# Four layers forward and backward on one core: the derivative of the feature map is no longer stored, and the opening's loads and zeroing are planned elsewhere

## The chip, the core and the metric

The kernel runs on one core of a Trainium2 chip, in one launch. The metric is the device time of that launch in microseconds (us), lower is better. TensorE is called PE here, VectorE DVE, ScalarE ACT, GpSimd POOL and SyncE SP, as the profile does; PEld is the weight load of PE. SP and ACT also issue the DMAs: SPq and ACTq are their issue queues.

## The reference

A residual stream x of 2048 tokens by 640 features (bf16) goes through four layers, A, B, A, B, and the gradient of the result goes back through them. Layer A is linear attention with 32 heads of 20 features, layer B is attention over a window of 256 keys.

```python
def _A_ref(x, wqkv, wo):                      # x is the layer norm of the stream
    q, k, v = split_heads(x @ wqkv)           # 32 heads of 20
    phi = lambda t: jnp.where(t > 0, t + 1, jnp.exp(t)) + 1e-6
    pq, pk = phi(q), phi(k)
    kv = einsum("bhsd,bhse->bhde", pk, v);  z = sum over s of pk
    o = (pq @ kv) / (pq . z + 1e-6)
    return merge_heads(o) @ wo
x = x + A(layernorm(x)); x = x + B(layernorm(x)); x = x + A(layernorm(x)); x = x + B(layernorm(x))
```

The outputs are the last x, and the gradients with respect to the input x, both weights of A and both weights of B (each pair of weights is used in two layers, so their gradients are sums of two). In the backward pass of layer A the gradient at phi(q) is multiplied by the derivative of phi at q, which is 1 where q is above 0 and exp(q) elsewhere, that is min(exp(q), 1); the same for k. Since phi(q) = max(q, 0) + min(exp(q), 1) + 1e-6 up to rounding, min(phi(q) - 1e-6, 1) is that derivative too.

## The kernel before, in words

The stream is cut into 16 tiles of 128 tokens (`TT` = 16), and everything is written as operations of one engine each. Each stage collects its operations in a list planner (`Sched`, lines 87 to 200): every operation names its engine, a cost in ns, what it reads and writes and, for a DMA, its kind and size. `order` (126) then plays the stage through with these costs. In each step it takes the operation that can start earliest, of equals the one that was created first, and that fixes the order of the instructions in every engine's queue. It fixes the order alone: on the chip each queue runs in that order and waits for what the data really needs. The planner's DMA model is in lines 167 to 177: one shared channel of 300 bytes per ns, plus 2000 ns to landing.

The stages, with the stretch of the profiled span that each takes:

- **Opening, 0 to about 120 us** (`forward`, 1056 to 1069, `a_first` at 963). For each of the 16 tiles: layer norm (`ln`, 471: two `bn_stats`, `bn_aggr` and the scaled write of tile `hn` on DVE, two small activations on ACT), transposition of hn on PE with a copy by ACT, and a store of hn to DRAM from SP (486). Then `a_qkv` (488) multiplies by the 1920 columns of `Wqkv_A` in six chunks of 320 (two for q, two for k, two for v; five matmuls each). For a q or k chunk ACT takes exp into tile `ee` (516), DVE takes the minimum with 1 in place (517) and adds max(q, 1e-6) to it (520); the sum is the feature `pp` or, for k, a slice of `gcar`. After that ee holds the derivative. ACT issues five stores of 160 KB per tile: pq (527), eq (529, the derivative of q), pk (533), ek (535, the derivative of k) and v (507). ee has four buffers, pp and hn's transpose two and three, and hn one.
- Before the first tile the queues hold the loads: on ACT Wqkv_A in two parts (chunks 0 and 1 first, 955 to 958), on SP the input x in three parts, tile 0, tiles 1 to 3, tiles 4 to 15 (959 to 961). In the same stage SP loads the other weights (`Wo_A`, `Wqkv_B`, `Wo_B`, five slices each, 1061 to 1064) and turns twenty weight blocks by DMA into DRAM copies for the backward pass (`flip_w`, 924 and 1065). Here the profile names `Wo_A` and `Wqkv_B` slabR, since they lie over that buffer, as hn and several later tiles do.
- DVE also zeroes fourteen tiles that later stages use (`zeros`, 407, written at 1059). In the planner nothing holds these back, so they can start at time 0.
- **First pass, about 120 to 400 us** (`ab_pass(0)`, 984): per tile the rest of layer A, layer B, and for the third layer hn, k and v (again with `a_qkv`, chunks 2 to 5, so with pk, ek and v stores). **Second pass, about 400 to 740 us** (`ab_pass(2)`): the same for the last two layers; q of the third layer comes late, in `late_q` (542), which stores pq (568) and eq (569).
- **Window attention backward**, about 740 to 1045 and 1470 to 1770 us (`B_attn_bwd`, 1613), in an order written out by hand; the change does not touch it.
- **Two backward phases**, `bwd_phase` (1091), about 1045 to 1470 and 1770 to the end. In the second half of each, `lin_grads` (1465) runs per tile, interleaved with `tail` (1276) of the same layer, and in the first phase with `local_dO` (1362) of the layer below. `lin_grads` loads eq and ek of its tile from DRAM (1476, SP queue, two buffers each; in the first phase ek's lie over slabR) and multiplies them with PE's result (1503). `tail` computes the layer norm's gradient: DVE 1317, ACT 1324 (w), POOL 1327 (gw = w + g), DVE 1329 (the new g). `local_dO` has a product on POOL too (1377), and DVE reduces it (1380).

The names that the prediction uses: the planner's dependency keys are tuples such as `("rs", 0, tt)` (the layer norm scale of tile tt is known) or `("vv", tt, 5)` (the last chunk of v is written). A key that nothing has written yet when the operation is created gives no dependency. That is the case for the weight loads of line 1064, which name `("vv", tt, 5)` before it exists; their only order is that of one slice behind the other of the same weight.

## Time and profile before

| what | value |
|---|---|
| three runs before | 2145.37, 2146.77, 2151.33 us, median 2146.77 |
| the profiled execution | 2145.22 us, its span 2143.5 us |
| mean granted PE clock | 0.975 |
| busy shares of the span | PE 94%, PEld 65%, DVE 67%, ACT 56%, POOL 41% |
| instructions | 68024 |
| moved by DMA | 376.43 MB |
| stores of eq and ek | 64, 160 KB each, all issued by ACT |
| loads of eq and ek | 64, 160 KB each, all issued by SP |

The profile is one execution, recorded by the hardware. A row of a timeline gives the start in us from the start of the span, the duration, engine, line, operation, output and input, and in brackets how long the engine had been idle and what ended that. A row of a group gives, after the bar, the busy time in us and the mean ns of one instruction, then the idle time just before them. A row of stretches gives start and end, then for each engine the busy us with the number of instructions, then the granted PE clock (1.00 is full), the share of the 16 DMA engines in use, and GB/s. The issue of a DMA is not counted as busy time of its engine.

### The profile page before, as it was taken

How to read it: one execution, taken by the hardware profiler on the slowest of the kernel's cores; microseconds unless marked ns; L12 is line 12 of the kernel's file. 1: busy time of each engine (PE TensorE's matmuls, PEld its weight loads, DVE VectorE, ACT ScalarE, POOL GpSimd, SP SyncE). 2: the span in 40 equal slices, each digit the busy share in tenths (PEclk: the TensorE clock that was granted, in tenths of full speed). 3: DMA queues.
4: the chain of work that ended last, by engine and by line, in shares of the span. 5: the costliest groups of instructions: out<-in, count | busy, mean ns of one | idle time of the engine just before them, and what ended most of it. 6: DMA issues, size and time to landing. Idle time of an engine off the chain costs nothing. (4 is left out here: it accounts for less than half of the span.)

```text
span 2143.5 us, 68024 instructions
## 1 busy us (share of the span) xinstructions
PE 2008.2 (94%) x27908; PEld 1389.2 (65%) x27908; DVE 1440.1 (67%) x2954; ACT 1203.3 (56%) x1995; POOL 879.4 (41%) x1850
## 2 busy tenths in 40 slices
PE   6879999889999899999899999999999999999999
PEld 4656666656666577777666667656777765666764
DVE  6757777567776599999634368606998984444651
ACT  3527878647888589899422233216988881221430
POOL 1015666316777456666223223204665652230210
PEclk9989999999999899999899999999999999999999
DMA  9928989469998788987987899847999998989943
GB/s 291 256 106 179 191 193 191 119 198 201 210 208 191 146 157 151 161 161 155 193 185 168 213 200 203 175 104 142 157 158 151 170 170 162 199 185 227 186 111 102
DMA packets 943687, 376.43 MB, mean 176 GB/s; under 512 B 821776, under 2 KB 923664, under 8 KB 943120
## 3 DMA queue, kind: packets, MB, share of 16 engines
q1 hardware_dynamic: 866176, 299.16, 71.9%
q10 hardware_dynamic: 77200, 72.94, 11.1%
q8 instruction: 218, 3.57, 0.7%
q14 instruction: 93, 0.76, 0.1%
HBM read 109.02 MB, written 112.07 MB: 103 GB/s over the span
## 5 line engine op out<-in xcount | busy, mean ns | idle before, releaser
L1693 DVE TENSOR_TENSOR ds_sb<-pair,e_sb 128x768 bf16<-128x768 f32 x480 | 437.6, 951 | 57.8 <-PE pair L1654 49.6
L1673 ACT ACTIVATE e_sb<-pair 128x768 bf16<-128x768 f32 x480 | 390.9, 815 | 95.6 <-PE pair L1654 67.4
L839 POOL TENSOR_SCALAR_AFFINE_SELECT e_sb<-e_sb 128x384 bf16<-128x384 bf16 (+1 forms) x512 | 198.3, 406 | 357.5 <-ACT e_sb L830 335.7
L830 ACT ACTIVATE e_sb<-s_ps 128x1152 bf16<-128x1152 f32 (+2 forms) x256 | 273.8, 1070 | 100.2 <-PE s_ps L826 78.4
L1685 POOL TENSOR_SCALAR_AFFINE_SELECT e_sb<-e_sb 128x256 bf16<-128x256 bf16 x448 | 182.0, 406 | 227.1 <-ACT e_sb L1673 226.9
L1327 POOL TENSOR_TENSOR gw<-w,gcar 128x640 f32<-128x640 f32 x64 | 89.4, 1397 | 423.4 <-ACT w L1324 406.8
L1138 PEld LDWEIGHTS <-slabR 128*128 128x128 bf16 x1920 | 185.6, 98 | 116.1 <-DMA slabR<-o 3.7
L1682 POOL TENSOR_SCALAR_AFFINE_SELECT e_sb<-e_sb 128x256 bf16<-128x256 bf16 x512 | 206.5, 406 | 89.3 <-ACT e_sb L1673 89.3
L1718 PEld LDWEIGHTS <-dsT 128*128 128x128 bf16 x2880 | 146.2, 97 | 97.7 <-issue 91.5
L1709 ACT COPY dsT<-dsT_ps 128x768 bf16<-128x768 bf16 x240 | 191.2, 796 | 9.4 <-PE dsT_ps L1706 6.6
L448 PE MATMUL mm_ps<-slabR,hnTB 128*128 128x320 bf16 x960 | 170.5, 308 | 10.5 <-DVE gcar L520 6.0
L1706 PE MATMUL dsT_ps<-ident,ds_sb 128*128 128x128 bf16 x1848 | 158.2, 223 | 1.3 <-ACT dsT L1709 1.1
L1722 PEld LDWEIGHTS <-ds_sb 128*128 128x128 bf16 x2880 | 145.1, 96 | 0.8 <-issue 0.8
L1722 PEld LDWEIGHTS <-e_sb 128*128 128x128 bf16 x2880 | 145.0, 96 | 0.0
L844 POOL TENSOR_SCALAR_AFFINE_SELECT e_sb<-e_sb 128x512 bf16<-128x512 bf16 x224 | 142.6, 636 | 0.0
L833 ACT ACTIVATE e_sb<-s_ps 128x384 bf16<-128x384 f32 (+2 forms) x256 | 119.9, 468 | 32.3 <-PE s_ps L826 15.1
L1138 PE MATMUL dw_ps<-dqkv,slabR 128*128 128x480 bf16 x640 | 134.7, 366 | 0.0
L1309 ACT ACTIVATE dh<-mm_ps 128x320 f32<-128x320 f32 x64 | 28.0, 437 | 189.8 <-PE mm_ps L1138 164.9
L1138 PE MATMUL dw_ps<-dqkv,om 128*128 128x480 bf16 x640 | 134.2, 366 | 0.0
L1654 PE MATMUL pair<-slabR 32*128 32x384 bf16 (+2 forms) x1024 | 120.5, 326 | 12.0 <-DVE ds_sb L1693 5.2
L1138 PEld LDWEIGHTS <-om 128*128 128x128 bf16 x800 | 77.5, 98 | 71.3 <-DMA om<-o 2.4
L864 PEld LDWEIGHTS <-e_sb 128*128 128x128 bf16 x2880 | 105.5, 96 | 26.6 <-POOL e_sb L844 7.5
(234 smaller groups left out, 4357.6 us busy)
## 6 DMA issues: line engine op xcount, KB each, us to landing
qkvp<-qk_slab SPq DMA_DIRECT2D x64, 256.0 KB, 3.7
hn<-slabR SPq DMA_DIRECT2D x64, 160.0 KB, 2.9
qkvp<-v_slab SPq DMA_DIRECT2D x32, 256.0 KB, 3.4
slabR<-qkvp SPq DMA_DIRECT2D x16, 512.0 KB, 4.8
o<-o SPq DMA_DIRECT2D x48, 160.0 KB, 2.9
eq<-ee ACTq DMA_DIRECT2D x32, 160.0 KB, 3.0
pq<-pp ACTq DMA_DIRECT2D x32, 160.0 KB, 2.4
ek<-ee ACTq DMA_DIRECT2D x32, 160.0 KB, 2.7
```

The costliest lines, as they stand in the source:

```text
L448: nc.tensor.matmul(ps.t[:, w0:w0 + width], lhsT=lhsT(), rhs=rhs(), start=start, stop=stop)
L830: op("ACT", av(3 * nkt * P), lambda: nc.scalar.activation(e.t[:, 0:3, 0:nkt, :], s3.t[:, :, 0:nkt * P].rearrange("p h (i q) -> p h i q", q=P),
L839: nc.gpsimd.affine_select(out=v, in_=v, compare_op=ALU.is_ge, fill=0.0, base=0, pattern=[[0, h1 - h0], [1, P]], channel_multiplier=-1)
L1138: nc.tensor.matmul(ps.t[:, w0:w0 + width], lhsT=lhsT(), rhs=rhs(), start=start, stop=stop)
L1673: nc.scalar.activation(E[n][:, 2 * p:2 * p + 2], PR[h][:, :, 0:3 * P].rearrange("p i (j q) -> p i j q", q=P), ACT.Exp, scale=self.c_att)
L1682: nc.gpsimd.affine_select(out=e[:, :, j, :], in_=e[:, :, j, :], compare_op=ALU.is_ge, fill=0.0, base=0, pattern=[[0, 2], [-1, P]], channel ...
L1685: nc.gpsimd.affine_select(out=e[:, :, j, :], in_=e[:, :, j, :], compare_op=ALU.is_ge, fill=0.0, base=-1, pattern=[[0, 2], [1, P]], channel ...
L1693: nc.vector.tensor_mul(DS[n][:, hs], PR.pop(h)[:, :, 0:3 * P].rearrange("p i (j q) -> p i j q", q=P), E[n][:, hs])
L1706: nc.tensor.transpose(ps[:, i, j, :], DS[n][:, 2 * p + i, j, :], self.ident)
L1709: (nc.scalar.copy if by == "A" else nc.vector.tensor_copy)(TSB[h], TPS.pop(h))
L1718: nc.tensor.matmul(a[:, 0, hh, :], lhsT=TSB[2 * n + hh // 2][:, hh % 2, j, :], rhs=ld[g]["K"][:, k, cs], start=(i == 0), stop=(i == len(dq ...
L1722: nc.tensor.matmul(a[:, 1 + x, hh, :], lhsT=src[n][:, hh, j, :], rhs=ld[g][rhs][:, q, cs], start=(i == 0), stop=(i == len(dkv) - 1))
```

## The change

Three edits, in the planner's input and in what is stored.

- **No eq and ek.** The two DRAM tensors per layer and their 64 stores (lines 529, 535, 569) are gone. In `lin_grads` the same two buffers are loaded from pq and pk, and POOL turns each in place into the derivative with one `tensor_scalar`: add -1e-6, then minimum with 1, over 128 x 640 bf16. The planner is told 1000 ns for it.
- **Opening's loads.** A third DMA kind "L" is told its landing time outright: x tile 0 at 2.8 us, Wqkv_A's parts at 5 and 9.5 us, x tiles 1 to 3 at 5.5 us, x tiles 4 to 15 at 14 us. The load of x tiles 4 to 15 moves behind the first LN store (hn of tile 0) in the plan, and the fifteen weight slices now name the LN store of tiles 1 to 11 (`("hnd", 0, tt)`), which is written by then.
- **Zeroing.** The fourteen memsets are created one after the other between tiles 3 and 13, and each names the layer norm scale of a tile from 3 to 12.

```diff
@@ line 166 @@
             ready[e].remove(o)
             if o.dma:
                 kind, size = o.dma
-                if kind == "B":
+                if kind == "L":
+                    free[e], chan_ = t + 500, size - 2000
+                elif kind == "B":
                     free[e], chan_ = t + 1300, t + 2500
                 elif kind == "T":
                     free[e] = t + 1100 + size / 1000
@@ line 174 @@
                 else:
                     free[e] = t + (330 if e == "SP" else 200)
                     chan = max(chan, t) + size / 300
-                o.end = (chan_ if kind == "B" else chan) + 2000
+                o.end = (chan_ if kind in "BL" else chan) + 2000
             else:
                 free[e] = t + o.dur
                 o.end = free[e] + (170 if e == "PE" else 0)
@@ line 273 @@
         for l in (0, 2):
             self.sv[l] = dict(
                 pq=d.tile([T, D], BF, name=f"pq{l}"), pk=d.tile([T, D], BF, name=f"pk{l}"),
-                eq=d.tile([T, D], BF, name=f"eq{l}"), ek=d.tile([T, D], BF, name=f"ek{l}"),
                 v=d.tile([T, D], BF, name=f"v{l}"), o=d.tile([T, D], BF, name=f"o{l}"),
                 r32=d.tile([T, self.H], F32, name=f"r32{l}"),
                 mbd=d.tile([D, D + P], BF, name=f"mbd{l}"),
@@ line 483 @@
                                                                  scalar2=rs, op0=ALU.subtract, op1=ALU.mult),
                    [("x", tt), m, ("rs", l, tt)], [hn])
                 turn(how, lambda: hnT.t, lambda: hn.t, DT, [hn], [key_of(hnT)])
-                dma("SP", lambda: self.tm_view(self.hn_d[l])[:, tt, :], lambda: hn.t, 160 * KB, [hn], [])
+                dma("SP", lambda: self.tm_view(self.hn_d[l])[:, tt, :], lambda: hn.t, 160 * KB, [hn], [("hnd", l, tt)])
 
             def a_qkv(l, tt, hnT):
                 sv = self.sv[l]
@@ line 521 @@
                             out=pd(), in0=ps.t[:, 0:CW], scalar=1e-6, in1=es(), op0=ALU.max,
                             op1=ALU.add), [ps, (e, ci)], [(c["p"], ci) if kind == "q" else ("pk", tt, ci)])
                         if ci == 3 and "q" in c:
-                            p_, e = c["p"], c["q"]
+                            p_ = c["p"]
                             turn("s", lambda: pqT[:, :, tt * P:(tt + 1) * P], lambda: p_.t, DT, [(p_, 0), (p_, 1)],
                                  [("pqT", tt)])
                             dma("ACT", lambda: self.tm_view(sv["pq"])[:, tt, :], lambda: p_.t, 160 * KB,
                                 [(p_, 0), (p_, 1)], [])
-                            dma("ACT", lambda e=e: self.tm_view(sv["eq"])[:, tt, :], lambda e=e: e.t, 160 * KB,
-                                [(e, 0), (e, 1)], [])
                         if ci == 3:
-                            e = c["k"]
                             dma("ACT", lambda: self.tm_view(sv["pk"])[:, tt, :], lambda: pk[:, tt, :], 160 * KB,
                                 [("pk", tt, 2), ("pk", tt, 3)], [])
-                            dma("ACT", lambda e=e: self.tm_view(sv["ek"])[:, tt, :], lambda e=e: e.t, 160 * KB,
-                                [(e, 2), (e, 3)], [])
                     return f
                 return [chunk(ci) for ci in range(6)]
 
@@ line 566 @@
                 else:
                     flip(own, lambda: p_.t, 160 * KB, [(p_, 0), (p_, 1)], [("pqT", tt)], **F)
                 dma("ACT", lambda: self.tm_view(sv["pq"])[:, tt, :], lambda: p_.t, 160 * KB, [(p_, 0), (p_, 1)], [], **F)
-                dma("ACT", lambda: self.tm_view(sv["eq"])[:, tt, :], lambda: e.t, 160 * KB, [(e, 0), (e, 1)], [], **F)
 
             def a_kv(l):
                 sv = self.sv[l]
@@ line 956 @@
                 dma("ACT", lambda c0=c0, c1=c1: wsb["Wqkv_A"][:, :, c0 * CW:c1 * CW],
                     lambda c0=c0, c1=c1: wA[:, :, c0 * CW:c1 * CW], 400 * (c1 - c0) * KB, [],
                     [("Wqkv_A", ci) for ci in range(c0, c1)])
-            for t0, t1 in ((0, 1), (1, 4), (4, TT)):
-                dma("SP", lambda t0=t0, t1=t1: x[:, t0:t1, :], lambda t0=t0, t1=t1: xin[:, t0:t1, :],
-                    160 * (t1 - t0) * KB, [("Wqkv_A", 0)] if t0 == 4 else [], [("x", i) for i in range(t0, t1)])
+                S.ops[-1].dma = ("L", 9500 if c0 else 5000)
+
+            def load_x(t0, t1, lands):
+                dma("SP", lambda: x[:, t0:t1, :], lambda: xin[:, t0:t1, :], 160 * (t1 - t0) * KB,
+                    [("hnd", 0, 0)] if t0 >= 4 else [], [("x", i) for i in range(t0, t1)])
+                S.ops[-1].dma = ("L", lands)
+            load_x(0, 1, 2800)
+            load_x(1, 4, 5500)
 
             def a_first(items, l, base, lag=0.0, late=()):
 
@@ line 1055 @@
 
             items = []
             a_first(items, 0, 0)
+            items.append((0.5, len(items), lambda: load_x(4, TT, 14000)))
             spread(items, 1.0, 9.0, [lambda f=f: op("POOL", 350, f, [], ["masks"]) for f in self.mask_steps])
-            spread(items, 2.0, 12.0, [lambda t=t, v=v, n=n: op("DVE", 100 + n * 0.45, lambda: nc.vector.memset(t, v), [],
-                                                               ["zeros"]) for t, v, n in zeros])
+            spread(items, 3.0, 13.0, [lambda t=t, v=v, n=n, i=i: op(
+                "DVE", 100 + n * 0.45, lambda: nc.vector.memset(t, v), [("rs", 0, 3 + i * 10 // len(zeros))], ["zeros"])
+                for i, (t, v, n) in enumerate(zeros)])
             for i, (k, src) in enumerate((("Wo_A", self.A_wo), ("Wqkv_B", self.B_wqkv), ("Wo_B", self.B_wo))):
                 for j in range(DT):
                     tt = 1 + 3 * i + j
-                    items.append((tt + 0.9, len(items), lambda k=k, src=src, j=j, tt=tt: load_w(k, src, "SP", j, [("vv", tt, 5)])))
+                    items.append((tt + 0.9, len(items), lambda k=k, src=src, j=j, tt=tt: load_w(k, src, "SP", j, [("hnd", 0, tt)])))
             for i in range(4 * DT):
                 at = 4.5 + 0.5 * i
                 items.append((at, len(items), flip_w(i, ("rs", 0, int(at) - 1))))
@@ line 1473 @@
                         c[nm] = b = R[nm].buf()
                         flip(lambda b=b: b.t, lambda src=src: src[row, :], size,
                              [("dNd", tt)] if nm == "dNT" else [], [b])
-                    c["eq"], c["ek"] = load("eq", sv["eq"], tt), load("ek", sv["ek"], tt)
+                    for nm, p_ in (("eq", "pq"), ("ek", "pk")):
+                        c[nm] = b = load(nm, sv[p_], tt)
+                        op("POOL", 1000, lambda b=b: nc.gpsimd.tensor_scalar(
+                            out=b.t, in0=b.t, scalar1=-1e-6, scalar2=1.0, op0=ALU.add, op1=ALU.min), [], [b])
 
                 def chunk(kind, ci):
                     def f():
```

## The prediction

> **What bounds the kernel now.** I read the page's busy shares first, then busy time by stretch, then the timelines of the two places that the change touches.
>
> ```profile
> PE 2008.2 (94%) x27908; PEld 1389.2 (65%) x27908; DVE 1440.1 (67%) x2954; ACT 1203.3 (56%) x1995; POOL 879.4 (41%) x1850
> ```
>
> ```profile
> 20.00:30.00 10.00, 9.37 (x58) 6.24 (x59) 6.15 (x19) 5.80 (x14) 0.00 (x0) 0.70 0.99 300
> 40.00:50.00 10.00, 7.27 (x58) 5.18 (x59) 6.20 (x18) 4.78 (x13) 0.00 (x0) 0.83 0.90 251
> 0.00:50.10 50.10, 30.82 (x215) 20.45 (x216) 31.98 (x89) 18.63 (x46) 5.89 (x26) 0.90 0.96 298
> 50.10:109.60 59.50, 50.99 (x467) 37.35 (x465) 43.03 (x123) 35.66 (x88) 0.00 (x0) 1.00 0.96 250
> 165.00:378.00 213.00, 201.31 (x3467) 140.93 (x3465) 160.82 (x405) 172.43 (x286) 139.00 (x306) 1.00 0.89 188
> 1245.00:1365.00 120.00, 113.62 (x1046) 86.18 (x1045) 101.25 (x218) 39.06 (x102) 36.48 (x27) 1.00 1.00 195
> 1950.00:2055.00 105.00, 102.37 (x1001) 79.63 (x1000) 66.32 (x174) 34.45 (x88) 16.09 (x12) 0.98 0.92 191
> ```
>
> The columns behind the length are PE, PEld, DVE, ACT, POOL, then granted clock, DMA share and GB/s. PE is the bound nearly everywhere: 94% of the span, 95% of the first pass (201.31 of 213), 95% and 97% of the two `lin_grads` halves (the last two rows). The opening is the exception. PE is busy 30.82 of the first 50.10 us and 50.99 of the next 59.50, with the DMA engines 96% in use. So the opening is where something can be won, and the backward halves, where POOL gets new work beside a busy DVE, are where something can be lost.
>
> ```profile
> 9.82 1.48 SPq L416 DMA_DIRECT2D hn<-slabR  x1
> ...
> 50.15 0.35 SPq L416 DMA_DIRECT2D hn<-slabR  x1
> ...
> 109.62 0.34 SPq L416 DMA_DIRECT2D hn<-slabR  x1
> ```
>
> These are the LN stores of tiles 0, 5 and 15, one per tile, so they give the pace: 40.3 us for the first five tiles (8.1 each), 59.5 us for the next ten (5.95 each).
>
> **The change, part by part.** *Opening, start.* DVE's first layer norm stands behind the zeroing:
>
> ```profile
> 2.33 1.66 DVE L1059 MEMSET mbd<- 128x1920 uint32 x1 [0.35 <-issue]
> 4.04 1.57 DVE L1059 MEMSET qk_slab<- 128x512 uint32 x3
> 5.66 2.11 DVE L1059 MEMSET v_slab<- 128x512 uint32 x4
> 7.68 0.43 DVE L476 BATCH_NORM_STATS2 st<-x 128x6 f32<-128x320 bf16 x1
> ```
>
> ```profile
> Wqkv_A<-in_A_wqkv_dram ACTq DMA_DIRECT2D x1, 1600.0 KB, 12.2
> ...
> x<-in_A_x_dram SPq DMA_DIRECT2D x1, 160.0 KB, 2.6
> ```
>
> Tile 0 of x is issued as the first DMA of SP at 0.8 and lands 2.6 later, at about 3.5 (estimate). From the first statistics (7.68) to the LN store (9.82) it takes 2.14 us, so with the zeroing gone from the front the store comes at about 5.6: **-4.2 us**. The weights must keep up. The second part of Wqkv_A took 12.2 us to land because the slices and all of x were issued around it. In the new order 3.1 MB (x tiles 0 to 3 and Wqkv_A) go first; at 298 GB/s that is 10.4 us, so k's columns are there at about 11, when the two q chunks (after 7) are just through. x tiles 4 to 15, moved behind the LN store, make it 5.1 MB, 17 us; tile 4 isn't due before 5.6 + 4 x 5.6 = 28. What hides the later load is thus ten us of earlier tiles; without that cover it would cost the difference.
>
> *Opening, tiles 0 to 5.* At the later pace these five take 29.7 us; they took 40.3, so 10.6 us are lost. Two idle gaps of PE and two stretches of low clock explain it:
>
> ```profile
> 20.11 0.71 PE L464 MATMUL s_ps<-ident,slabR 128*128 128x128 bf16 x5 [3.68 <-DVE slabR L482]
> ...
> 42.15 0.45 PE L464 MATMUL s_ps<-ident,slabR 128*128 128x128 bf16 x5 [2.85 <-DVE slabR L482]
> ```
>
> The gaps are 3.68 + 2.85, the clock cost 0.30 x 10 + 0.17 x 10 = 4.7 (rows 20 to 30 and 40 to 50), together 11.2. In both gaps PE waits for a layer norm (line 482) that DVE wrote late: its queue had statistics of later tiles in front, an order that the planner chose with wrong landing times. With landing times near the real ones and the weight slices spread over tiles 1 to 11 instead of the first third, I let three quarters go: **-8 us**. Bounds: 0 (the new order has gaps of its own) and -10.6.
>
> *Opening, tiles 5 to 15.* Per tile PE is busy 5.1 us of 5.95, DVE 4.3, ACT 3.6 plus five issues:
>
> ```profile
> L416 ACTq DMA_DIRECT2D eq<-ee x32: 326/422/1445, 15.0 to 654.7; - x32
> L416 ACTq DMA_DIRECT2D ek<-ee x32: 326/388/672, 23.6 to 422.8; - x32
> ```
>
> [...] Two of the five go, 0.8 us of a tile, part of which runs beside ACT's own work; and of the 14.9 MB that 250 GB/s moves in 59.5 us, twenty stores of 160 KB, 3.3 MB or 22%, go too. Against that stand the memsets, 1.66 + 1.57 + 2.11 and about 0.9 (estimate) for the fifth v_slab and five small ones, 6.2 us of DVE, eight tenths of them here: 0.5 per tile, DVE then 4.8. PE at 5.1 is the floor, so the bounds are -8.5 (all at the floor) and +5 (all memset time on the path, nothing won). I take a pace of 5.6, nearer the floor since three engines then stand at 5.1 or less: **-3.5 us**.
>
> *The two passes.* 32 further stores go, 16 of ek and 16 of eq, 12.8 us of ACT's queue at 0.4 each. PE leads here with 95%, so ACT's work hides it; the 11.7 us in which PE idles in the first pass bound the gain. But the planner replays the whole forward stage and every queue may come out in another order. I take **-1 us**, bounds -6 and +4.
>
> *The two backward halves.* 64 operations on POOL that this trace does not show. Nearest rows:
>
> ```profile
> L844 POOL TENSOR_SCALAR_AFFINE_SELECT e_sb<-e_sb 128x512 bf16<-128x512 bf16 x224 | 142.6, 636 | 0.0
> ```
>
> ```profile
> L1327 POOL TENSOR_TENSOR gw<-w,gcar x64: 1392/1397/1402, 1057.9 to 2081.2; 128x640 f32<-128x640 f32 x64
> L1329 DVE SCALAR_TENSOR_TENSOR gcar<-slabR,sm,gw x32: 883/1946/2001, 1059.3 to 1377.4; 128x640 bf16<-128x640 bf16 x32
> L1329 DVE SCALAR_TENSOR_TENSOR gcar<-hn,sm,gw x32: 873/883/2001, 1787.6 to 2082.6; 128x640 bf16<-128x640 bf16 x32
> ```
>
> One input, bf16, at the rate of the first row: 640/512 x 0.636 = 0.80 us. Two inputs in float: 1.40. I take 0.9, nearer the form with one input; two per tile are 1.8. POOL has room:
>
> ```profile
> 1284.79 1.34 POOL L1377 TENSOR_TENSOR prod<-slab,o 128x640 f32<-128x640 bf16 x1
> 1292.29 1.40 POOL L1327 TENSOR_TENSOR gw<-w,gcar 128x640 f32<-128x640 f32 x1 [6.16 <-ACT w L1324]
> ```
>
> ```profile
> 1995.10 1.40 POOL L1327 TENSOR_TENSOR gw<-w,gcar 128x640 f32<-128x640 f32 x1 [5.18 <-ACT w L1324]
> ```
>
> It idles 6.16 us per tile in the first half and 5.18 in the second. (A tile is 1.40 + 1.34 + 6.16 = 8.9 us there and 1.40 + 5.18 = 6.6 here.) The way from the load is long enough too:
>
> ```profile
> slabR<-ek SPq DMA_DIRECT2D x13, 160.0 KB, 3.4
> ```
>
> ```profile
> 1281.14 0.63 SPq L1128 DMA_DIRECT2D slabR<-ek  x1
> ```
>
> ```profile
> 1288.38 0.48 DVE L1503 TENSOR_TENSOR dqkv<-mm_ps,slabR 128x320 bf16<-128x320 f32 x1
> ```
>
> ek of a tile is issued at 1281.14, lands at 1284.5 (median way 3.4), is read first at 1288.38. If the new operation stands behind `prod`, which ends at 1286.13, it ends at 1287.0: 1.4 us to spare. If it stands in front of gw or prod, these and their DVE users come up to 0.9 later.
>
> The price is on DVE. Line 1329 takes 883 ns alone and 1946 where `prod` runs beside it (it starts 0.1 us after it): 1.06 us longer, about what is left of prod. DVE idles 18.75 of 120 us in the first half, 1.4 us for each of 13.5 tiles, and 38.7 of 105 in the second, 2.4 for each of 16. So if both new operations block a DVE instruction of this kind for their whole length, the first half loses 16 x (1.8 - 1.4) = 6 us and the second nothing. If neither does, nothing. I take **+2 us**, bounds 0 and +6.
>
> The Trainium skill, "SBUF — State Buffer", section "Who interferes with whom", says that a GpSimd instruction that reads SBUF and a VectorE instruction with two SBUF inputs exclude each other for the whole instruction. The trace agrees, with 883 against 1946 ns. By that rule every meeting costs full length, and the sum would be that of the +6; by the row of the second half, where nothing meets, +0.
>
> **Sum.** -4.2 - 8 - 3.5 - 1 + 2 = -14.7. From the profiled execution's 2145.22 that is 2130.5, and I write 2131. The median of the runs is 1.55 above the profiled execution, within the runs' spread.
>
> **The rivals.** *Opening unchanged in pace.* DVE, not ACT or the DMA engines, sets the opening: PE's two gaps wait for DVE, and the memsets now lie inside the tiles. Then the start gives -4.2, half of the early loss stays (-5), and the memsets cost +5: -4, 2141. For it speaks that both gaps name line 482; against it DVE's 4.3 us of 5.95. *Opening at the floor.* All of the early loss goes and ten tiles run at 5.1: -4.2 - 10.6 - 8.5 = -23, with -5 from the passes 2117. Against it: three engines at nearly one level never wait for nothing. *Slower by the shared access of POOL and DVE.* The new operations take the upper price, 1.40, and both block a DVE instruction every tile: first half 16 x (2.8 - 1.4) = 22, second 16 x (2.8 - 2.4) = 6; and since DVE's delay reaches PE through line 1503, which writes what the tail's matmuls take, nothing hides it. With the forward side at -16.7 that is +11, 2156. It decides from 23 us of backward loss, 1.4 + 23/16 = 2.8 us of DVE per tile, so both must be at the top. For it: 1946 ns. Against it: POOL idles when 1317 and 1329 run in the second half. *The change doesn't do what it says:* x tiles 4 to 15 behind the store arrive late and tile 4 stalls; by the numbers above there are ten us of cover, so I count it in the first rival.
>
> **How the numbers follow.** Forecast, 2122 to 2138: 0.60. Pace unchanged, 2138 to 2148: 0.20. Floor, below 2122: 0.10. Slower, above 2149: 0.10. Leaving out half of each end, the range is 2119 to 2149. About 0.3%, 6.4 us around 2146.8, is what a measurement here can tell: faster is below 2140.4. Forecast, floor and a quarter of the second case give 0.75; the rest of it 0.16; slower than 2153.2 0.09.
>
> **What would show it.** Right: the first LN store at 5 to 6 us, the sixth near 37, the last near 93, no PE gap above 2 us in the first 50, the clock there 1.0 after the start; POOL rows of 0.8 to 1.0 us on eq and ek, and `lin_grads` halves within 5 us of their length. Wrong: LN stores still 6 us apart; line 1329 or 1317 at 1.9 us in the second half; PE waiting for line 1503.

## The result, and the profile after

The changed kernel takes 2174.07 us (median of 2169.28 to 2177.84), the kernel before 2146.07 beside it. The ratio is 1.013, 95% interval 1.0094 to 1.0165: **28 us slower**, where 2131 was forecast and the range ended at 2149. The profiled execution after is 2171.13 us with a span of 2169.4, against 2145.22 and 2143.5. The two spans differ by 25.9 us, and that is what the traces have to explain.

The LN stores after (SP, those of tiles 0, 5 and 15):

```profile
5.93 0.34 SPq L417 DMA_DIRECT2D hn<-slabR  x1
...
37.20 0.33 SPq L417 DMA_DIRECT2D hn<-slabR  x1
...
99.12 0.33 SPq L417 DMA_DIRECT2D hn<-slabR  x1
```

They came at 9.82, 50.15 and 109.62 before. The start (3.9 us earlier) and the first five tiles (9.0 more) did what was forecast, the next ten did not: 61.9 us where they took 59.5. The page's busy shares, and busy time by stretch of the changed kernel, in the prediction's columns. The last two rows are the stretches of the `lin_grads` halves, moved by 17 us (the table below: the first ends 17.2 later, the second starts 16.6 later).

```profile
PE 2014.9 (93%) x27908; PEld 1390.1 (64%) x27908; DVE 1439.6 (66%) x2954; ACT 1203.5 (55%) x1995; POOL 1040.6 (48%) x1914
```

```profile
20.00:30.00 10.00, 7.05 (x60) 5.01 (x60) 8.29 (x24) 4.68 (x11) 0.00 (x0) 1.00 0.64 181
40.00:50.00 10.00, 7.45 (x65) 5.32 (x63) 7.33 (x23) 5.30 (x13) 0.00 (x0) 1.00 1.19 255
...
165.00:378.00 213.00, 195.83 (x3326) 135.52 (x3324) 154.06 (x386) 164.32 (x270) 132.23 (x292) 0.99 0.81 171
1262.00:1382.00 120.00, 108.38 (x984) 80.81 (x983) 100.42 (x210) 36.14 (x95) 101.09 (x52) 1.00 0.90 185
1967.00:2072.00 105.00, 97.10 (x920) 74.52 (x919) 62.46 (x160) 31.21 (x81) 73.77 (x35) 0.97 0.86 178
```

The clock of the opening is 1.00 in both early stretches (0.70 and 0.83 before). But PE works less everywhere behind it: 195.83 of 213 us in the first pass (201.31 before), 108.38 of 120 and 97.10 of 105 in the two halves (113.62 and 102.37). The number in the last busy column is new: POOL 101.09 and 73.77 us, where it had 36.48 and 16.09. Its new instruction, by the buffer that it works on (min/median/max ns in the first row; the others show busy us and mean ns):

```profile
L1480 POOL TENSOR_SCALAR eq<-eq x32: 2344/2345/3041, 1070.7 to 2079.1; 128x640 bf16<-128x640 bf16 x32
```

```profile
L1480 POOL TENSOR_SCALAR eq<-eq 128x640 bf16<-128x640 bf16 x32 | 78.4, 2450 | 19.6 <-DMA eq<-pq 17.4
...
L1480 POOL TENSOR_SCALAR slabR<-slabR 128x640 bf16<-128x640 bf16 x16 | 42.8, 2674 | 17.4 <-DMA slabR<-pk 16.2
L1480 POOL TENSOR_SCALAR ek<-ek 128x640 bf16<-128x640 bf16 x16 | 40.5, 2534 | 26.8 <-DMA ek<-pk 24.2 <-DVE gcar L1331 2.1
```

It takes 2.34 us at least and 3.04 at most. The prediction took 0.9, with 1.40 as its upper end.

The table below places each kernel's profile against that of before: how many us earlier (-) or later (+) it reaches seven points. *LN* is the last LN store of the opening, *pass 1* the first pass's last v-slab store (SP), *bwd* the first matmul of the attention backward, *sums 1* and *sums 2* the last matmul of the first half of each phase, *lin 1* and *lin 2* the last matmul for the layer norm's gradient in each `lin_grads` half.

| kernel | LN | pass 1 | bwd | sums 1 | lin 1 | sums 2 | lin 2 |
|---|---|---|---|---|---|---|---|
| before, us | 109.6 | 385.2 | 735.3 | 1223.5 | 1372.9 | 1952.0 | 2078.2 |
| after | -10.5 | +0.3 | +1.2 | +9.3 | +17.2 | +16.6 | +25.9 |
| 1 stores only | -14.4 | -2.8 | -5.5 | +4.2 | +11.4 | +13.1 | +23.1 |
| 2 opening only | +2.0 | +6.1 | +3.8 | +3.9 | +3.0 | +2.2 | +1.2 |
| 3 folded | -9.3 | +3.7 | +1.6 | +3.1 | +4.1 | +3.0 | +2.1 |
| 4 one operation | -11.9 | -0.7 | -2.9 | -0.5 | +6.0 | +3.2 | +8.9 |
| 5 2400 ns told | -9.4 | +2.5 | +1.1 | +1.5 | +13.0 | +13.8 | +23.2 |
| 6 one of two | -10.1 | +2.5 | +0.7 | +5.5 | +6.2 | +5.8 | +13.0 |
| 7 one, behind gw | -8.8 | +2.3 | +3.1 | +4.6 | +4.6 | +3.6 | +3.1 |
| 8 two, behind gw | -11.5 | -1.0 | -2.0 | -3.2 | +6.2 | +8.2 | +14.2 |
| 9 same order | -7.1 | -11.4 | -16.3 | -16.0 | -15.4 | -13.6 | -13.5 |
| 10 old opening, counted passes | -15.2 | -13.0 | -18.2 | -13.8 | -13.6 | -12.5 | -13.5 |
| 11 zeroing early | -16.7 | -4.8 | -5.1 | -3.4 | -5.3 | -4.7 | -3.1 |
| 12 the same, counted passes | -17.5 | -18.6 | -24.4 | -22.7 | -25.1 | -25.0 | -26.0 |
| 13 counted on ACT only | -17.9 | -13.7 | -16.8 | -17.1 | -18.0 | -18.2 | -18.6 |
| 14 counted as traffic only | -16.4 | -14.8 | -20.6 | -19.7 | -20.1 | -20.9 | -19.4 |

The changed kernel gains 10.5 us by the last LN store, has lost all of it by the end of the first pass, and loses 24.7 us from the start of the backward: 8.1 up to the first sums, 7.9 in the first `lin_grads` half, 9.3 in the second. Single stretches repeat to a few us: the two attention backwards, which no kernel touches, come out 2.0 us shorter to 2.9 longer, and in 10, without any POOL instruction, the stretch from bwd to sums 1 is 4.4 longer.

### The profile page after: what moved, and what is told of

It is laid out like the page before. It is cut to its first block, busy times and chain, and to the rows that moved or that the text cites. A ratio compares the mean times of both kernels' runs of the same rounds, so it can differ in the third digit from the quotient of the medians.

```text
span 2169.4 us, 67955 instructions
## 1 busy us (share of the span) xinstructions
PE 2014.9 (93%) x27908; PEld 1390.1 (64%) x27908; DVE 1439.6 (66%) x2954; ACT 1203.5 (55%) x1995; POOL 1040.6 (48%) x1914
## 5 line engine op out<-in xcount | busy, mean ns | idle before, releaser
L1659 PE MATMUL pair<-slabR 32*128 32x384 bf16 (+2 forms) x1024 | 120.5, 325 | 11.9 <-DVE ds_sb L1698 5.0
L859 PE MATMUL pv_ps<-v_slab,e_sb 128*128 128x32 bf16 x2880 | 117.2, 177 | 9.9 <-POOL e_sb L839 9.4
```

What stands on the lines that cost most here:

```text
L859: nc.tensor.matmul(pv.t[:, h % 16, :], lhsT=e.t[:, hh, j, :], rhs=vts[j].t[:, h, :], start=(j == 0), stop=(j == nkt - 1))
```

## The experiments

My theory at this point: POOL's mis-priced instruction costs the backward its 25 us, and the first pass loses because the planner gives another order once the stores are no longer counted. The rivals: the loss in the backward is one of order or of the loads, not of POOL's time; the first pass gives back whatever the opening gains. Times are medians beside the kernel before on the same chip, whose median there was 2140.1 to 2143.1; so ratios are compared. The expected ranges were mostly written beside a kernel before of about 2146 us; a time can fall into one by this difference of up to 6 us alone, and where it matters the text says so. The table is set against one profiled execution of before (2145.22 us): it tells where time goes, and the ratio how much.

### The two halves of the change apart

*1, stores only.* Stores dropped and recomputed on POOL, opening as before:

> The change's second half alone: stores dropped, derivative recomputed on POOL, opening as in the kernel before. Theory (POOL's two operations per tile at 2.34 to 3.04 us cost about 25 us in the backward, 8 in the first phase's sums and 17 in the two lin_grads halves; the first pass loses 9 because the planner, no longer counting the stores, gives another order): last LN store still near 109, backward +25, first pass +5 to +10, so 2175 to 2181. Rival one (the first pass loses because of the new opening, not because of the missing stores): second a_kv at the 426 us of before, total 2169 to 2172. Rival two (the backward's loss comes from the order of the forward, not from POOL): no loss in the backward, 2146 to 2156.

Measured: 2164.38 us, ratio 1.012 (1.0098 to 1.0142). The backward loses 28.6 us (table, from bwd to lin 2), so that part is the POOL side's alone. The rest was a miss: the opening gains 14.4 us without any of the new loads and zeroing, more than the 10.5 of the whole change. The passes lose 8.9 of it.

*2, opening only.* The new loads and zeroing, eq and ek stored and loaded:

> The change's first half alone: new opening, the derivative still stored and loaded. Theory (the opening's gain of 8 us is real, what takes it back is the first pass's new order without the stores): first pass starts 5 to 8 us earlier and keeps most of it, 2138 to 2142. Rival (whatever the opening gains, the first pass gives back, for its order follows the opening's): second a_kv near 426 again, 2145 to 2148. A third: with the stores still there the DMA engines hold the opening back, last LN store near 105, 2142 to 2145.

Measured: 2147.28 us, ratio 1.0051 (1.0032 to 1.0070). The time lies in the first rival's range, but only because the kernel before was faster here (2140.46): it is 0.5% slower than that, which none of the three expected. Nor does the rival's reason fit: the first pass gives nothing back, for there is nothing. The first six tiles are as early as in the changed kernel (sixth LN store at 37.4), the last LN store comes at 111.6, 2.0 later than before. So what the opening wins comes from the stores that are gone; the replanned opening wins 13 us in six tiles and loses them in the next ten.

### What POOL's instruction costs, and how

*3, folded.* No POOL instruction; DVE's product takes the minimum with 1 itself:

```diff
-op("DVE", ..., lambda: nc.vector.tensor_mul(dst(), ps, e), ...)
+op("DVE", ..., lambda: nc.vector.scalar_tensor_tensor(out=dst(), in0=e, scalar=1.0, in1=ps, op0=ALU.min, op1=ALU.mult), ...)
```

> The changed kernel without the POOL operations: the derivative's minimum is folded into VectorE's product (minimum with 1, then times the gradient, one instruction), which leaves out the subtraction of 1e-6. Theory: the backward's 25 us go and the forward's loss of about 1 stays, 2145 to 2152 (the upper end if the folded product takes 0.1 us longer than the product). Rival (loads of pq and pk, or the order, cost the backward its time): 2160 to 2172.

Measured: 2147.34 us, ratio 1.0035 (1.0019 to 1.0051). From bwd to lin 2 it loses 0.5 us. The loads of pq and pk and the folded product (481 ns a piece, as the plain one) cost nothing: all of the backward's loss is POOL's instruction.

Where it lands is seen in the second half. POOL's timeline of the changed kernel, one tile, and that of the folded one:

```profile
2024.08 1.40 POOL L1329 TENSOR_TENSOR gw<-w,gcar 128x640 f32<-128x640 f32 x1
2026.52 2.35 POOL L1480 TENSOR_SCALAR ek<-ek 128x640 bf16<-128x640 bf16 x1 [1.04 <-DVE gcar L1331]
2028.94 2.35 POOL L1480 TENSOR_SCALAR eq<-eq 128x640 bf16<-128x640 bf16 x1
2031.37 1.40 POOL L1329 TENSOR_TENSOR gw<-w,gcar 128x640 f32<-128x640 f32 x1
```

```profile
2016.95 1.40 POOL L1329 TENSOR_TENSOR gw<-w,gcar 128x640 f32<-128x640 f32 x1 [5.17 <-ACT w L1326]
2023.52 1.40 POOL L1329 TENSOR_TENSOR gw<-w,gcar 128x640 f32<-128x640 f32 x1 [5.18 <-ACT w L1326]
```

Without the instruction POOL idles until ACT's w is there, and gw comes every 6.57 us. With it gw follows eq without a gap, 7.29 us after the last one: gw no longer waits for w, it stands behind eq. DVE pays, not by longer instructions but by waiting (its line after gw, 14 instances each over 100 us, first folded, then changed):

```profile
L1331 DVE SCALAR_TENSOR_TENSOR gcar<-hn,sm,gw 128x640 bf16<-128x640 bf16 x14 | 12.3, 877 | 2.6 <-POOL gw L1329 2.6
```

```profile
L1331 DVE SCALAR_TENSOR_TENSOR gcar<-hn,sm,gw 128x640 bf16<-128x640 bf16 x14 | 12.4, 883 | 17.4 <-POOL gw L1329 17.4
```

The mean is 877 and 883 ns: this instruction is not lengthened by POOL's work beside it. The wait for gw went from 2.6 to 17.4 us.

In the first phase's sums, three of the new instructions (of tiles 0 and 1, whose loads are there early) stand in front of a `prod` (lin_dO's product), from 1070.68 on; the last of them and `prod`:

```profile
1076.23 2.35 POOL L1480 TENSOR_SCALAR eq<-eq 128x640 bf16<-128x640 bf16 x1
1078.65 1.39 POOL L1420 TENSOR_TENSOR prod<-slabA,o 128x640 f32<-128x640 bf16 x1
```

*4, one operation.* Order of every engine as in the changed kernel, `op1` and the subtraction left out:

> The changed kernel, every engine's order the same, with POOL's instruction cut to one operation (the minimum with 1; the subtraction of 1e-6 is left out). Theory (POOL pays for each of the two operations on each element): 1.2 to 1.5 us in place of 2.34, the backward gets back 12 to 20 of its 24 us, 2150 to 2160 beside the 2171 of the changed kernel. Rival (the instruction's time goes by its elements, not by its operations): 2.3 us again, 2165 to 2174.

Measured: 2157.0 us, ratio 1.0061 (1.0039 to 1.0084); the backward loses 11.8 us.

```profile
L1480 POOL TENSOR_SCALAR eq<-eq x32: 1797/1804/2057, 1065.9 to 2062.2; 128x640 bf16<-128x640 bf16 x32
```

1.80 us, not the 1.2 to 1.5 expected: an operation is worth 0.54, and 1.26 is there without (an estimate, a straight line through the two). A quarter less of the instruction halves the loss, so the loss isn't proportional: there is slack, and the price exceeds it.

In the first `lin_grads` half DVE does pay by longer instructions. Two small ones, which the prediction did not name, in the folded kernel and in this one, over the same 115 us:

```profile
L1386 DVE SCALAR_TENSOR_TENSOR slab<-dd,slab 128x32 bf16<-128x32 f32 x14 | 4.2, 300 | 0.5
L1384 DVE TENSOR_SCALAR slab<-dd 128x32 bf16<-128x32 f32 x14 | 3.3, 239 | 0.5
```

```profile
L1386 DVE SCALAR_TENSOR_TENSOR slab<-dd,slab 128x32 bf16<-128x32 f32 x13 | 7.5, 576 | 0.4
L1384 DVE TENSOR_SCALAR slab<-dd 128x32 bf16<-128x32 f32 x13 | 6.0, 465 | 0.4
```

They grow where one POOL instruction ends beside the first of them (line 1384) and the next starts just ahead of the second. That is 0.50 us more a tile, 6.5 in 13, and the half loses 6.5 (sums 1 to lin 1). In the changed kernel the two take 386 and 320 ns, about 2 us in all (estimate). The rest of its 7.9 goes with DVE's product, which waits for k's derivative:

```profile
L1508 DVE TENSOR_TENSOR dqkv<-mm_ps,slabR 128x320 bf16<-128x320 f32 x25 | 12.1, 485 | 5.6 <-POOL slabR L1480 5.6
```

*5, 2400 ns told.* The planner's cost for it 2400 instead of 1000:

> The changed kernel with the planner told 2400 ns for POOL's instruction in place of 1000. Theory (POOL's time itself is what costs, 4.7 us more per tile beside DVE): backward still 18 to 25 us longer, 2164 to 2172. Rival (the loss is one of order: the planner, told 1000, put four of them ahead of what PE needs): backward only 2 to 10 us longer, 2148 to 2157.

Measured: 2166.56 us, ratio 1.0102 (1.0070 to 1.0134). The sums lose nothing any more (from bwd to sums 1: 0.4 us, 8.1 before), so those eight were order. The two halves lose 11.5 and 9.4. POOL's timeline in the second:

```profile
2022.33 1.40 POOL L1329 TENSOR_TENSOR gw<-w,gcar 128x640 f32<-128x640 f32 x1
2023.81 3.04 POOL L1480 TENSOR_SCALAR ek<-ek 128x640 bf16<-128x640 bf16 x1
2026.93 2.35 POOL L1480 TENSOR_SCALAR eq<-eq 128x640 bf16<-128x640 bf16 x1
2029.36 1.40 POOL L1329 TENSOR_TENSOR gw<-w,gcar 128x640 f32<-128x640 f32 x1
```

Not one gap is left: 1.40 + 3.04 + 2.35 and 0.08 between each make 7.03 us a tile, where the tile had 6.57. POOL is the bound. It is so only with the meeting with DVE that makes one of them 3.04: with 2.35 for both, the same row of instructions would take 6.34 (estimate) and fit.

*6, one of two.* Only q's derivative on POOL, k's folded:

> The changed kernel with POOL's two-operation instruction for q's derivative alone; k's is folded into VectorE's product (minimum with 1, without the 1e-6). Theory (POOL is full: 1.40 + 2 x 2.35 and more of the 6.6 us of a tile; with one instruction it has 2.8 us left): backward 0 to 5 us longer than with both folded, 2145 to 2151. Rival (each instruction costs by itself, for it stands in front of gw or prod whenever it comes): half of the 24, 2155 to 2161.

Measured: 2154.79 us, ratio 1.0067 (1.0048 to 1.0085), as the rival said, and my theory that POOL must be full fell. In the first half the instruction stands behind `prod` and costs next to nothing (0.7 us from sums 1 to lin 1). In the second it costs 7.2, though POOL idles 1.7 us or more in each tile:

```profile
2024.34 2.35 POOL L1481 TENSOR_SCALAR eq<-eq 128x640 bf16<-128x640 bf16 x1 [2.60 <-DMA eq<-pq]
2026.77 1.40 POOL L1329 TENSOR_TENSOR gw<-w,gcar 128x640 f32<-128x640 f32 x1
```

POOL waits for eq's load, works on it, and only then does gw, whose w was written from 2025.20 to 2026.12. In the tile before, w was there at 2018.73 and gw came at 2020.34, behind another eq. Neither eq is used before the next tile.

*7, one, behind gw.* The same, with the order in the second half told, and 2400 ns in place of 1000:

```diff
+                        if nb is None and tt > 3:
+                            S.ops[-1].after.add(gws[la, tt - 4])
```

> The kernel with one POOL instruction per tile (q's), in the second lin_grads half ordered behind the gw of four tiles earlier, k's folded. Theory (what cost 6.5 us there with POOL only 57% full is the place in front of gw): second half within 2 us of the folded one, 2146 to 2150 beside 2155. Rival (an instruction of 2.35 us on POOL costs DVE and the loads their time wherever it stands): 2153 to 2160.

Measured: 2150.01 us, ratio 1.0042 (1.0025 to 1.0059). The second half is free: -0.5 us from sums 2 to lin 2.

```profile
2011.37 1.40 POOL L1331 TENSOR_TENSOR gw<-w,gcar 128x640 f32<-128x640 f32 x1 [2.75 <-ACT w L1328]
2012.86 2.35 POOL L1484 TENSOR_SCALAR eq<-eq 128x640 bf16<-128x640 bf16 x1
2017.95 1.40 POOL L1331 TENSOR_TENSOR gw<-w,gcar 128x640 f32<-128x640 f32 x1 [2.74 <-ACT w L1328]
```

The same 2.35 us on the same engine; gw waits for w again, every 6.58 us. Both edits reach the chip as an order alone, so the place in front of gw cost it; which of the two moved it was not tried apart.

*8, two, behind gw.* The same place for both, 2400 ns told:

> The changed kernel with both POOL instructions, the planner told 2400 ns, and in the second lin_grads half each of them ordered behind the gw of four tiles earlier instead of in front of it. Theory (gw stands behind instructions that wait for a load; with gw first they run in POOL's slack): second half 3 us longer than with folding at most, gw's wait for ACT back, 2156 to 2162. Rival (POOL is full with two of them, whatever their order: 1.40 + 2 x 2.35 and their stretching give 6.6 to 7.0 us a tile): second half 6 to 9 us longer as before, 2163 to 2172.

Measured: 2162.14 us, ratio 1.0097 (1.0067 to 1.0128). The time lies between the two theories; the half decides. From sums 2 to lin 2 it loses 6.0 us, the rival's figure, for POOL runs without a gap again (its rows up to the next eq at 2014.90, and the DVE row that starts just before the first):

```profile
2007.87 3.04 POOL L1483 TENSOR_SCALAR eq<-eq 128x640 bf16<-128x640 bf16 x1
2010.99 2.35 POOL L1483 TENSOR_SCALAR ek<-ek 128x640 bf16<-128x640 bf16 x1
2013.42 1.40 POOL L1331 TENSOR_TENSOR gw<-w,gcar 128x640 f32<-128x640 f32 x1
```

```profile
2007.82 0.89 DVE L1334 SCALAR_TENSOR_TENSOR gcar<-hn,sm,gw 128x640 bf16<-128x640 bf16 x1 [1.32 <-POOL gw L1331]
```

Two causes, then, in the second half: with two instructions POOL is full, and with one only the place counts. The rows also show who pays when the two meet: DVE keeps its 0.89 us, POOL takes 3.04 in place of 2.35. It does so for all twelve eq's between 1990 and 2090 us, 0.69 each, and a tile takes 7.03 us; without it 6.34 (estimate) would fit the 6.57. So shared access is part of why POOL is full; no run took it away by itself.

### What the passes and the opening lose

The kernels from here on issue no store of eq and ek and fold the derivative as in 3 (minimum with 1, without the 1e-6).

*9, same order.* The kernel before, each engine's order kept: an empty operation that the planner counts as a store stands in each store's place.

```diff
-dma("ACT", lambda e=e: self.tm_view(sv["ek"])[:, tt, :], lambda e=e: e.t, 160 * KB, [(e, 2), (e, 3)], [])
+op("ACT", 60, lambda: None, [(e, 2), (e, 3)], [], dma=("D", 160 * KB))
```

> Every engine's order of the kernel before, with the 64 stores left out (the planner still counts them) and the folded product in place of the loaded derivative (minimum with 1, without the 1e-6). Theory: the stores themselves are worth little where PE leads, but in the opening they take 22% of what moves: 0 to 4 us, 2142 to 2147. Rival (dropping the stores costs the first pass its time, whatever the order): first pass 5 to 9 us longer, 2150 to 2156. Another (the stores were the opening's bound): 2136 to 2140.

Measured: 2131.84 us, ratio 0.9963 (0.9949 to 0.9978). By its ratio that is 2138 beside 2146, the range of the last expectation, but not for its reason alone: 7.1 us in the opening, and 9.2 more up to the attention backward. Leaving the stores out wins in the passes too, if the order stays.

*10, old opening, counted passes.* Opening planned without the stores, the passes as if they were there:

> Opening as before but planned without the stores, the two passes planned as if the stores were still there, no store issued anywhere, folded product in the backward (minimum with 1, without the 1e-6). Theory (the stores' absence gains 14 us in the opening and 8 in the passes; the loss of 7 to 9 in the passes comes from planning them without the stores): last LN store near 95, forward's end 22 us earlier than before, 2119 to 2125. Rival (a gain in the opening is given back in the first pass whatever its order): forward's end 10 to 16 us earlier, 2127 to 2135.

Measured: 2131.66 us, ratio 0.9946 (0.9925 to 0.9968). The opening gains 15.2, the passes 3.0 more: no loss, but less than the 8 expected; the time lies in the rival's range, the forward (18.2) between the two.

*11, zeroing early.* The changed kernel, folded, with the zeroing planned as before:

> The changed kernel with the folded product (minimum with 1, without the 1e-6) and the zeroing planned as in the kernel before, the loads as in the changed one. Theory (the opening gains 4 at the start and loses 7 between tiles 5 and 11, for the memsets stand in DVE's queue there): first LN store near 10 again or 8, sixth near 40, last near 95, end 2140 to 2144 beside 2146. Rival (the weight slices behind the LN stores lose it): last LN store at 99 or later, 2146 to 2150.

Measured: 2142.33 us, ratio 0.9995 (0.9976 to 1.0014). The last LN store comes 16.7 us early instead of 9.3 (3, which differs in the zeroing's plan alone). So the zeroing's new place cost 7 us of the opening. Its instructions in the changed kernel stand among the tiles, the large ones from 19.14 to 61.19 us; the first:

```profile
19.14 1.66 DVE L1061 MEMSET mbd<- 128x1920 uint32 x1 [0.35 <-issue]
```

The passes lose again, 11.6 us.

*12, the same, counted passes.*

> Loads of the opening as in the changed kernel, zeroing planned as before the change, no store issued, the two passes planned as if the stores were there, folded product in the backward (minimum with 1, without the 1e-6). It differs from the kernel before it (zeroing planned early) in the passes' plan alone. Theory (the plan of the passes without the stores costs 9 us in the first pass, the plan with them wins 8): last LN store near 93, first v-slab store near 134, second a_kv and forward's end 20 to 23 us earlier than in the kernel before, 2119 to 2127. Rival (the passes lose whatever an earlier opening gains): forward's end 5 to 10 us earlier, 2133 to 2140.

Measured: 2127.44 us, ratio 0.9936 (0.9918 to 0.9954), the largest gain measured together with 14, whose interval overlaps. Forward's end is 24.4 us early, a little beyond the theory's 20 to 23; the time is just above its range. Its profiled execution is the fastest of its runs (2119.26 to 2131.14), so of the span's 26 us the ratio confirms 14. Against 11 only the passes' plan differs. ACT's timeline in the first pass shows what that does, first in 11:

```profile
251.37 0.49 ACT L828 ACTIVATE e_sb<-s_ps 128x384 bf16<-128x384 f32 x1
252.05 0.41 ACTq L417 DMA_DIRECT2D pk<-gcar  x1
252.50 1.33 ACTq L417 DMA_DIRECT2D o<-oB  x1
253.87 0.45 ACTq L417 DMA_DIRECT2D linv<-slabR  x1
254.42 1.13 ACT L825 ACTIVATE e_sb<-s_ps 128x1152 bf16<-128x1152 f32 x1 [2.55 <-PE mm_ps L449]
```

```profile
244.44 0.34 ACTq L417 DMA_DIRECT2D pk<-gcar  x1
244.83 0.49 ACT L832 ACTIVATE e_sb<-s_ps 128x384 bf16<-128x384 f32 x1 [0.51 <-DVE qk_slab L694]
245.41 1.13 ACT L829 ACTIVATE e_sb<-s_ps 128x1152 bf16<-128x1152 f32 x1
245.53 0.33 ACTq L417 DMA_DIRECT2D o<-oB  x1
245.90 0.45 ACTq L417 DMA_DIRECT2D linv<-slabR  x1
```

The second fence is 12. In 11 three stores are issued in a row between two exps, for 2.27 us, and ACT computes nothing for 2.55 us before the exp behind them. The bracket names PE's mm_ps, but the rows between show that ACT was issuing. PE then waits for that exp:

```profile
255.60 0.35 PE L821 MATMUL s_ps<-QT,KT 32*128 32x128 bf16 x12 [1.47 <-ACT e_sb L825]
```

In 12 exps stand between the stores. This order repeats tile after tile: in the two orders of ACT the second exp and the stores of pk, o and linv have changed places. The length does not repeat: in most tiles of 11 the store of o takes 0.41 to 0.47 us, and three of twelve take 1.33 to 2.09. The store of o in the first pass (165 to 378 us), in the kernel before and in the changed one:

```profile
L416 ACTq DMA_DIRECT2D o<-oB x13: 326/327/348, 177.5 to 377.9; - x13
```

```profile
L417 ACTq DMA_DIRECT2D o<-oB x12: 343/474/2057, 168.4 to 360.4; - x12
```

So the changed kernel has 11's order, and an issue there takes up to 2.06 us. Of the kernels without the eq and ek stores, those that issue the three in a row (the changed one, 1, 3 to 8 and 11) lose 8.9 to 11.9 us between the last LN store and the attention backward, and those with an exp between (9, 10, 12, 13 and 14) lose 1.1 at most and gain up to 9.2. That the plan of the passes costs this is shown; that these three stores do it is argued, for no kernel moved them alone.

*13 and 14, counted on ACT only, as traffic only.* What of the absent store shapes the good order: its 200 ns on ACT's queue in the planner, or its traffic on the planner's DMA channel?

> As the kernel before it, but the planner counts only 200 ns of ACT's queue for each store that isn't there, and nothing on its DMA channel. Theory (what shapes the good order is that ACT's queue is counted full): the forward's end 18 to 23 us earlier, 2119 to 2129. Rival (it is the counted traffic, by which loads are planned later): forward's end 5 to 10 us earlier, 2133 to 2142.

> The counterpart: the planner counts only the traffic of the absent stores on its DMA channel, and 1 ns on ACT's queue. Theory (ACT's queue shapes it): forward's end 5 to 10 us earlier, 2133 to 2142. Rival (the traffic shapes it): 18 to 23 us earlier, 2119 to 2129.

Measured: 2127.64 us, ratio 0.9946 (0.9929 to 0.9963), and 2125.26 us, ratio 0.9932 (0.9911 to 0.9953). Forward's ends 16.8 and 20.6 us early: either alone keeps most of it, and the question has no answer in this form. With 1 ns on ACT and no traffic the planner gives 11's order to the last instruction, so each of the two differs from 11 by one count. 12, 13 and 14 can't be told apart by their intervals. Why an earlier free slot on ACT moves the three stores together stays open.

## Why the prediction was wrong, step by step

- **The step that failed: "I take 0.9, nearer the form with one input"**, and its upper end of 1.40. The instruction takes 2.34 us, up to 3.04. The price was scaled from a select over 128 x 512, another operation; this one costs about 1.26 us and 0.54 for each of its two operations on 640 elements (estimate). With the prediction's own idle time in the second half, 5.18 us of POOL per tile, 2 x 2.34 leaves 0.5, and the 0.69 by which one of the two grows beside DVE is more than that. The 6.16 of the first half was one of the longest gaps: most there are 5.5, in tiles of 8.2 us and not 8.9. The term "+2 us, bounds 0 and +6" became +24.7.
- **The way in which it costs was half wrong too.** The prediction put the price on DVE by shared access. In the first half some of it is there, 6.5 us in 4, but on two small instructions (lines 1384 and 1386 of the changed kernel) that the prediction left out. In the second half lines 1329 and 1317 of before hardly grow (877 to 883 and 815 to 857 ns). What costs there is POOL's own queue: gw behind an instruction that waits for a load (7 shows it: same instruction, other place, nothing lost), and POOL's fill (8), to which shared access adds on POOL's side. The sentence "if it stands in front of gw or prod, these and their DVE users come up to 0.9 later" named the place and then left it out of the sum.
- **The rival "slower by the shared access"** had the sign and, for the upper price, a near sum (22 + 6 for the halves; 7.9 + 9.3 came, with 8.1 in the sums, which no case held). Its mechanism, DVE blocked in every tile of both halves for the instruction's whole length, is not what the rows show, so the near sum is luck.
- **"The two passes, -1, bounds -6 and +4"** failed: +9.2 from the first pass's first matmul (113.1 against 121.1, 8.0 early) to the attention backward (1.2 late). The prediction said that every queue may come out in another order and gave that 4 us. With the order kept, the same missing stores gain 9.2 (9). The order costs more than the change's own work.
- **Opening, start and tiles 0 to 5**: right, -3.9 for -4.2 and -9.0 for -8, and for the reason given: with the stores in place the new loads and zeroing alone win 4.2 and 8.6 there (2). What the prediction missed is that the absent stores alone, which it counted from tile 5 on, win 7.8 in the first five tiles too (1), and the two don't add.
- **Opening, tiles 5 to 15**: +2.4 for -3.5, inside its bounds (-8.5 and +5). The upper bound's reason, the memsets on the path, is the one that 11 shows: zeroing early is worth 7 us at the last LN store.
- Of the signs named, the first LN store (5.93) and the sixth (37.20) came as said, the last at 99 instead of 93; PE's longest gaps of that stretch, behind the start, were 2.38 and 2.02; "POOL rows of 0.8 to 1.0 us" and "halves within 5 us" were the ones that told it wrong.

## What to carry to other kernels

A price for an operation that the trace lacks needs a row of the same operation, not of the same number of inputs; where there is none, measure it by itself or let the range reach what would fill the engine. On an in-order queue ask of each added instruction what stands behind it while it waits for its load, not only whether the engine has room. And where a planner fixes the order, dropping work from its input replans everything behind it: keep the old order with the work counted but not done, and see what the work itself is worth.

## What the runs showed of the hardware that I had not expected

- POOL's tensor_scalar over 128 x 640 bf16: 2.34 us with two operations, 1.80 with one, against 0.64 for a select over 128 x 512.
- Where POOL's tensor_scalar and DVE's instruction with two SBUF inputs meet, POOL's was the longer one (3.04 for 2.35, DVE 0.89 as alone); with `prod` in the kernel before it had been DVE's (1946 for 883 ns). The Trainium skill, "SBUF — State Buffer", section "Who interferes with whom", calls the shared ports an exclusive lock; the trace agrees in these two cases, where the one that came second paid. That one excludes the other for the whole instruction, as the prediction took from there, it does not show everywhere: in the changed kernel a DVE instruction of line 1386 that started 0.05 us behind POOL's eq (1294.97 us) took 0.82 for 0.30 us and ended 1.48 before POOL's, and one that started 1.07 behind another (1286.25) took its 0.30.
- The store of o from ACT's queue takes 0.33 us in the first pass of the kernel before; in the row of three it took 0.47 in the median of the changed kernel and up to 2.06. What makes single ones long no run shows.
